# A recurrent attention and mixture-of-experts kernel: three more evictions move from ScalarE to VectorE in the start-up

## The chip, the cores and the metric

The kernel runs on one core of one Trainium2 chip. The metric is the time of one execution on the device in microseconds (us), as the median of the runs that were timed. Lower is better.

## The reference, cut to what matters

```python
def _attn_ref(r, k, v, w, a, b):          # (4, 8, 768, 40): 32 heads, 768 steps, 40 wide
    for t in range(S):
        y[:, :, t] = np.einsum('bhd,bhde->bhe', rt, state)
        Sa = np.einsum('bhde,bhe->bhd', state, at)
        state_decay = state * wt[:, :, None, :] - np.einsum('bhd,bhe->bhde', Sa, bt)
        state = state_decay + np.einsum('bhd,bhe->bhde', vt, kt)
...
def _moe_ref(x, w_gate, w_output_gate, w1, w2):   # 3072 tokens, 8 experts
    e_idx = np.argmax(x @ w_gate, axis=1)
    for e in range(E):
        mask = e_idx == e
        h = np.maximum(x[mask] @ w1[e], 0.0)
        out[mask] = gate_w[mask, None] * eom[mask, e, None] * (h @ w2[e])
```

The first part is a recurrence over 768 steps for 32 heads, the second part routes each of the 3072 resulting tokens to one of eight experts.

## The kernel before

The 768 steps are cut into 12 chunks of 64 steps. Within a chunk the recurrence is written as a triangular system, so a chunk c goes through three stages.

**Prep(c).** `scan` (line 103) forms running products P and I of the decays with two scans on VectorE (line 116) and squares the decays on ScalarE (line 119, only for a range test). `prep` (line 137) scales the inputs: Av on VectorE or GpSimd (lines 184, 185), KBt on VectorE (line 212), Am from Av (line 201 on ScalarE, line 203 on GpSimd, or by DMA on line 192). Then line 225 multiplies KBt by Am on TensorE into PSUM tiles named pl, of which there are two buffers. For each of two sides (16 head pairs each) there are three groups, g0 = 0, 2 and 4, and so six pl tiles to a chunk. Each pl tile is evicted to SBUF in three pieces: the upper half of N (32 partitions, full rows of 64), the lower half of N (32 partitions, half rows) and LA (line 238). The upper half is on VectorE on line 234 for chunk 0, and on ScalarE on line 236 for all other chunks; the lower half is always on ScalarE, line 236. GpSimd then masks LA (line 240). KBt is also transposed on TensorE (line 163) and copied to KB by ScalarE (line 165); the next chunk's KBt may be written only after that.

**Tinv(c)** (line 251) inverts the triangular blocks of N on VectorE, in a long row of small multiplications and sums. Chunks 0 and 1 are done singly: the stage begins with a transposition of N on line 266 and ends with another on line 330, whose result ScalarE copies to Tc (line 333). From chunk 2 on, two chunks are done at once, from line 271 to line 336.

**Crit(c, q) and tail(c, q)** use Tc for the state update and the output, for two halves q of the heads. Their products on TensorE (lines 379 and 392) alternate with moves from PSUM on ScalarE (line 383) and, for chunks 0 and 1, with two additions on VectorE after each product with Nm (line 405).

The program is written in one stream, in which prep and tinv run ahead of crit. The framework's scheduler then sets the order on each engine from estimates of its own, before anything runs. Each engine takes its queue strictly in that order, so an instruction that waits holds up all behind it. After the attention the experts run, where TensorE is the busiest engine.

Of the kernel before, what the change touches and what calls it, by code (L numbers as in the profile page):

```python
# [49 lines left out]
def pat(x, off, dims):  # L50

    return bass.AP(x.tensor, x.offset + off, [x.ap[0]] + [list(d) for d in dims])


class Att:
# [47 lines left out]
    def scan(s, c):  # L103

        nc, V = s.nc, s.nc.vector
        n = 12 * 2 * 33
        w = s.p1.tile([120, n + 1], F32, name="w")
        V.memset(w[:, n:], 0.0)
        nc.sync.dma_start(out=w[:, 0:n], in_=s.win[c])
        s.D = s.p1.tile([120, 12, 3, C], F32, name="D")  # L110
        s.mark[c] = nc.sync.dma_start(out=s.D, in_=s.din[c]).ins
        P, I = (s.p1.tile([120, 12, 2, 33], F32, name=x) for x in "PI")
        Pf, If = (x.rearrange("p r h t -> p (r h t)") for x in (P, I))
        with s.tc.issue_after(s.mark['t', 0]) if c == 2 else ExitStack():
            for o, d in ((Pf, w[:, 0:n]), (If[:, ::-1], w[:, n:0:-1])):
                V.tensor_tensor_scan(out=o, data0=d, data1=s.rst, initial=0.0, op0=ALU.mult, op1=ALU.add)
        wq = pat(w, 1, [(33, 24), (1, 32)])
        with s.tc.issue_after(s.mark['n', 0]) if c == 1 else ExitStack():
            nc.scalar.activation(out=wq, in_=wq, func=AF.Square, bias=s.wb, accum_out=s.wsq[:, c:c + 1])
        rq = s.p1.tile([120, 24], F32, name="rq", bufs=2)  # L120
        V.reciprocal(out=rq, in_=P[:, :, :, 32])
        I3 = I.rearrange("p r h t -> p (r h) t")
        V.tensor_tensor(out=I3, in0=I3, in1=rq.unsqueeze(2).broadcast_to([120, 24, 33]), op=ALU.mult)
        s.Q = P, I, rq
# [12 lines left out]
    def prep(s, c):  # L137
# [45 lines left out]
        with s.tc.issue_after(s.mark['r', 0]) if c == 1 else ExitStack():  # L183
            (g if c > 1 else V).tensor_tensor(out=Av[:, :, 0:33], in0=a[:, :, 0:33], in1=I[:, :, 1, ::-1], op=ALU.mult)
            (g if c > 1 else V).tensor_tensor(out=Av[:, :, 33:64], in0=a[:, :, 33:64], in1=P[:, :, 0, 1:32], op=ALU.mult)
        with s.tc.issue_after(s.mark['n', 0]) if c == 1 else ExitStack():
            nc.scalar.copy(out=Av[:, :, 64:66], in_=P[:, :, :, 32])
        Ag = Av.rearrange("p (a g) t -> p a g t", a=2)
        if c and c != 2:
            for j in range(3):  # L190
                r, n = slice(40 * j, 40 * j + 40), 6 if j < 2 else 4
# [26 lines left out]
        for side in range(2):  # L218
            Am = s.Am[:, side]
            yield  # L220
            for g0 in range(0, 6, 2):
                pl = s.ps.tile([128, 2, 3, C], F32, name="pl", tag="pl" if c or g0 == 0 else "tl", bufs=2 if c or g0 == 0 else 3)
                nj = 3 if g0 < 4 else 2
                for i in range(2):
                    nc.tensor.matmul(pl[:, i, 0:nj], KBt[:, 6 * side + g0 + i].rearrange("p n t -> p (n t)"), Am[:, g0 + i:g0 + i + 6 * nj - 5:6, 0:64],  # L225
                                     start=True, stop=True)
                pv = pl.rearrange("p g j t -> p j g t")
                for h in range(2):
                    r = slice(64 * side + 32 * h, 64 * side + 32 * h + 32)
                    n = C - 32 * h  # L230
                    nn = pat(N[r], C * g0, [(6 * C, nj), (C, 2), (1, n)])
                    pn = pv[64 + 32 * h:96 + 32 * h, 0:nj, :, C - n:]
                    if c == 0 and not h:
                        V.tensor_scalar(out=nn, in0=pn, scalar1=-1.0, scalar2=None, op0=ALU.mult)
                    else:
                        s.mark['n', c] = nc.scalar.activation(out=nn, in_=pn, func=AF.Copy, scale=-1.0).ins  # L236
                la = pat(LA[64:128, side], 66 * g0, [(396, nj), (66, 2), (1, 64)])
                nc.scalar.activation(out=la, in_=pv[0:64, 0:nj], func=AF.Copy, scale=-1.0)  # L238
                for i in range(2):
                    g.affine_select(out=la[:, :, i], in_=la[:, :, i], pattern=[[0, nj], [1, C]], base=0, channel_multiplier=-1,  # L240
                                    compare_op=ALU.is_gt, fill=0.0)
                yield
# [344 lines left out]
class Moe:  # L587
# [346 lines left out]
    def experts(s, ctx, verdict):  # L934
# [21 lines left out]
        def unit(e, t0, nt, prep):  # L956

            for _ in s.expert(nt, W[e], T[e, t0], lambda: s.hp, ps1, ps2) if (e, t0) != (0, 0) else s.E0:
                next(prep, None)
            for _ in prep:  # L960
                pass
# [199 lines left out]
```

## Time and profile before

| | |
|---|---|
| median of 3 runs | 682.52 us (681.66 to 682.61) |
| the profiled execution's own time | 678.98 us |
| span of its trace, first to last instruction | 677.2 us |
| TensorE, matmul busy | 630.9 us (93%) |
| VectorE busy | 464.9 us (69%) |
| ScalarE busy | 340.2 us (50%) |
| GpSimd busy | 233.8 us (35%) |

The page cuts the span into 40 slices of 17 us. In the first 20 or so VectorE is mostly at 6 to 9 tenths and in the later ones at 4 to 6; the attention fills the first 427 us and the experts the rest. The granted TensorE clock is full but for slices 2 to 5, and one each in the middle and at the end. Shares over the whole span mix these stages, so the change has to be read from the first 135 us, where it lies.

In the views, PE is TensorE (PEld its weight load), DVE is VectorE, ACT is ScalarE, POOL is GpSimd and SP the queue that issues most DMAs.

### The profile page before, as it was taken

Reading aid. Unit: us, or ns where it says so; the run is one execution under the profiler, and the core shown is the slowest. Engines: PE = TensorE matmul, PEld = TensorE weight load, DVE = VectorE, ACT = ScalarE, POOL = GpSimd, SP = SyncE. Lnnn points to the kernel's source line nnn. Section 1 sums busy time; section 2 is a strip of 40 time slices with the busy share of each in tenths; the row PEclk is TensorE's granted clock in tenths of the full one; section 3 lists DMA queues with packets and bytes.
Section 4 is the critical chain, followed back from the end, with each engine's and each line's share of the span. In section 5 each row is a group of like instructions: output and inputs, shape, how many; then the busy total and the mean of one; then the engine's idle time right before and its main releaser. Section 6 shows DMA issues by size and latency. Waiting matters only on the chain. (4 is left out here: it accounts for less than half of the span.)

```text
span 677.2 us, 21154 instructions
## 1 busy us (share of the span) xinstructions
PE 630.9 (93%) x8871; PEld 564.3 (83%) x8871; DVE 464.9 (69%) x911; ACT 340.2 (50%) x783; POOL 233.8 (35%) x337
## 2 busy tenths in 40 slices
PE   7787988898999999989999889899999999999996
PEld 6475877787988888878889779799999999999985
DVE  8868689969986997699399654374774545654231
ACT  2577762784378357637743354253573435343120
POOL 9655321341144258314204111335342333211112
PEclk9667999999999999999999979999999999999999
DMA  5995763276346726643224752263774344431001
GB/s 141 179 184 132 175 156 82 78 165 168 98 128 166 157 80 168 173 97 99 83 80 126 194 165 76 58 195 85 213 203 152 115 135 134 150 103 34 19 11 32
DMA packets 56305, 84.45 MB, mean 125 GB/s; under 512 B 26848, under 2 KB 43515, under 8 KB 54763
## 3 DMA queue, kind: packets, MB, share of 16 engines
q1 hardware_dynamic: 52331, 74.05, 42.3%
q0 software_dynamic: 3872, 8.97, 4.7%
q8 instruction: 72, 1.18, 0.7%
q14 instruction: 30, 0.25, 0.1%
HBM read 67.59 MB, written 8.96 MB: 113 GB/s over the span
## 5 line engine op out<-in xcount | busy, mean ns | idle before, releaser
L863 DVE SCALAR_TENSOR_TENSOR hl<-ph,hh 128x480 fp32r<-128x480 f32 (+1 forms) x74 | 41.3, 567 | 65.4 <-ACT hh L862 65.3
L862 ACT ACTIVATE hh<-ph 128x480 fp32r<-128x480 f32 (+1 forms) x74 | 36.7, 501 | 93.5 <-PE ph L858 93.1
L878 POOL DMA_INDIRECT out_dram<-y,ti x32 | 34.3, 1073 | 141.5 <-DVE y L877 80.8
L873 PE MATMUL po<-w2h,hh 128*120 128x320 f32 x256 | 78.3, 311 | 0.2 <-ACT hh L862 0.2
L874 PE MATMUL po<-w2l,hh 128*120 128x320 f32 x256 | 77.6, 309 | 0.0
L858 PE MATMUL ph<-xh,w1h 128*128 128x480 f32 (+1 forms) x222 | 76.1, 347 | 0.3 <-DVE mem L704 0.3
L858 PE MATMUL ph<-xl,w1h 128*128 128x480 f32 (+1 forms) x222 | 75.7, 344 | 0.0
L875 PE MATMUL po<-w2h,hl 128*120 128x320 f32 x256 | 74.9, 308 | 0.0
L225 PE MATMUL pl<-Am,KBt 120*128 120x192 f32 (+1 forms) x288 | 62.9, 352 | 7.7 <-ACT LA L238 6.2
L240 POOL TENSOR_SCALAR_AFFINE_SELECT LA<-LA 64x192 f32<-64x192 f32 x144 | 55.2, 418 | 40.2 <-ACT LA L238 38.8
L383 ACT ACTIVATE As<-pa,hq 128x320 f32<-128x320 f32 x80 | 42.1, 528 | 47.2 <-PE pa L392 36.0
L236 ACT ACTIVATE N<-pl 32x192 f32<-32x192 f32 (+1 forms) x138 | 51.6, 374 | 26.3 <-PE pa L392 12.2
L225 PEld LDWEIGHTS pl<-Am,KBt 120*128 120x128 f32 x288 | 47.1, 205 | 13.4 <-ACT LA L238 8.7
L480 PE MATMUL pY<-KB,M 128*64 128x64 f32 (+1 forms) x768 | 53.3, 225 | 3.0 <-DVE M L468 3.0
L479 PE MATMUL pY<-Sd,R 128*64 128x64 f32 (+1 forms) x704 | 53.9, 227 | 0.0
L392 PE MATMUL pa<-As,Tc 64*32 64x40 f32 x1792 | 51.1, 204 | 2.9 <-ACT As L383 2.1
L730 POOL DMA_INDIRECT tab<-rec,si x24 | 29.9, 1245 | 67.6 <-DMA tab<-rec,si 45.5
L464 PE MATMUL pM<-R,VU 128*128 128x128 f32 x384 | 52.3, 287 | 0.9 <-ACT VU L456 0.8
L480 PEld LDWEIGHTS pY<-KB,M 128*64 128x64 f32 x768 | 46.9, 138 | 6.6 <-DVE M L468 3.4
L838 POOL DMA_INDIRECT xg<-xd,ti x32 | 35.8, 1118 | 44.6 <-PE px L821 32.7
L392 PEld LDWEIGHTS pa<-As,Tc 64*32 64x32 f32 x1792 | 40.3, 112 | 12.8 <-issue 3.8
L858 PE MATMUL ph<-xh,w1l 128*128 128x480 f32 (+1 forms) x148 | 50.7, 344 | 0.0
(198 smaller groups left out, 1571.2 us busy)
## 6 DMA issues: line engine op xcount, KB each, us to landing
D<-in_din_dram SPq DMA_DIRECT2D x12, 1080.0 KB
st<-in_w_dram SPq DMA_DIRECT2D x16, 512.0 KB
st<-in_w_dram SPq DMA_DIRECT2D x16, 480.0 KB
XS<-in_vt_dram SPq DMA_DIRECT2D x24, 256.0 KB
XU<-in_vt_dram SPq DMA_DIRECT2D x24, 256.0 KB
VU<-in_vl_dram SPq DMA_DIRECT2D x24, 208.0 KB
w<-in_win_dram SPq DMA_DIRECT2D x12, 371.2 KB
st<-in_w_dram SPq DMA_DIRECT2D x16, 256.0 KB
```

Source lines behind the costliest of these rows:

```text
L225: nc.tensor.matmul(pl[:, i, 0:nj], KBt[:, 6 * side + g0 + i].rearrange("p n t -> p (n t)"), Am[:, g0 + i:g0 + i + 6 * nj - 5:6, 0:64], sta ...
L236: s.mark['n', c] = nc.scalar.activation(out=nn, in_=pn, func=AF.Copy, scale=-1.0).ins
L240: g.affine_select(out=la[:, :, i], in_=la[:, :, i], pattern=[[0, nj], [1, C]], base=0, channel_multiplier=-1, compare_op=ALU.is_gt, fill=0.0)
L383: s.mark['as'] = nc.scalar.activation(out=x, in_=pa, func=AF.Copy, scale=s.hq[:, h:h + 1]).ins
L392: nc.tensor.matmul(pa[o + w:o + w + 32, i], m(p)[o:o + 64], x[o:o + 64, i, :], start=start, stop=True, tile_position=(o, o + w), skip_grou ...
L464: nc.tensor.matmul(pM[:, i], VU[:, h0 + i].rearrange("p n t -> p (n t)"), R[:, :, h0 + i], start=True, stop=True)
L479: nc.tensor.matmul(o, R[:, side, i, :], Sf[:, 40 * i:40 * i + w], start=True, stop=False)
L480: s.mark['y'] = nc.tensor.matmul(o, Ms[i // 4][:, i % 4, side, :], Kf[:, k:k + w], start=not c, stop=True).ins
L858: nc.tensor.matmul(ph, l, r, start=(i == 0), stop=(i == 7))
L873: nc.tensor.matmul(po, hh[f][:, ts_], w2h[:, f], start=(f == 0), stop=False)
L874: nc.tensor.matmul(po, hh[f][:, ts_], w2l[:, f], start=False, stop=False)
L875: nc.tensor.matmul(po, hl[f][:, ts_], w2h[:, f], start=False, stop=(f == 7))
```

## The change

The condition on line 233 is widened: the upper halves of N are evicted by VectorE for all six tiles of chunk 0 as before, and now also for the three tiles of chunk 1's second side (side 1). The two other edited lines write the same condition in another form and give the same marks.

```diff
-                    if c == 0 and not h:
+                    if not h and (c == 0 or c == 1 and side >= 1):
                         V.tensor_scalar(out=nn, in0=pn, scalar1=-1.0, scalar2=None, op0=ALU.mult)
                     else:
                         s.mark['n', c] = nc.scalar.activation(out=nn, in_=pn, func=AF.Copy, scale=-1.0).ins
```

Three instructions change engine, but the scheduler lays out everything after them anew. The order on all engines differs from chunk 1's second side to about chunk 5, and is the same again afterwards. Three places matter for what follows.

The first is VectorE's queue around chunk 1's second side. The rows with N from pl in 128 columns (32x3x128, 32x2x128) are upper halves; line 266 starts chunk 1's tinv; lines 121 and 123 belong to chunk 2's scan. Before:

```order
L121 RECIPROCAL rq<-P 120x24
L123 TENSOR_TENSOR I<-I,rq 120x792
L108 MEMSET w 120x1
L405 TENSOR_TENSOR As<-As,pa 32x320 x2
L266 STREAM_TRANSPOSE tmpf<-N 128x16x32
L267 TENSOR_SCALAR tmpf<-tmpf,hm 128x256
L268 SCALAR_TENSOR_TENSOR Ns<-tmpf,hm 128x16x16
L276 TENSOR_TENSOR tmpf<-Tt,Ns 128x2
```

And now:

```order
L121 RECIPROCAL rq<-P 120x24
L234 TENSOR_SCALAR N<-pl 32x3x128
L123 TENSOR_TENSOR I<-I,rq 120x792
L234 TENSOR_SCALAR N<-pl 32x3x128
L108 MEMSET w 120x1
L405 TENSOR_TENSOR As<-As,pa 32x320 x2
L234 TENSOR_SCALAR N<-pl 32x2x128
L266 STREAM_TRANSPOSE tmpf<-N 128x16x32
L267 TENSOR_SCALAR tmpf<-tmpf,hm 128x256
L268 SCALAR_TENSOR_TENSOR Ns<-tmpf,hm 128x16x16
L212 TENSOR_TENSOR KBt<-D,P 120x24x32
L212 TENSOR_TENSOR KBt<-D,I 120x24x32
```

The three evictions stand among chunk 2's scan work, each waiting for its product, and chunk 2's KBt has moved ahead of the tinv's first steps.

The second is ScalarE's queue in the same place. The rows 32x3x2x32 and 32x2x2x32 are lower halves, the last group's being 32x2x2x32; line 201 writes a part of Am for chunk 2. Before:

```order
L119 ACTIVATE w,wsq<-w,wb 120x24x32
L383 ACTIVATE As<-pa,hq 128x320
L181 ACTIVATE rs,rqm<-rq 120x24
L236 ACTIVATE N<-pl 32x3x128
L236 ACTIVATE N<-pl 32x3x2x32
L238 ACTIVATE LA<-pl 64x3x2x64
L236 ACTIVATE N<-pl 32x2x128
L236 ACTIVATE N<-pl 32x2x2x32
L238 ACTIVATE LA<-pl 64x2x2x64
L201 ACTIVATE Am<-Av,hj 120x2x6x64
```

And now:

```order
L119 ACTIVATE w,wsq<-w,wb 120x24x32
L383 ACTIVATE As<-pa,hq 128x320
L181 ACTIVATE rs,rqm<-rq 120x24
L236 ACTIVATE N<-pl 32x3x2x32
L238 ACTIVATE LA<-pl 64x3x2x64
L236 ACTIVATE N<-pl 32x3x2x32
L238 ACTIVATE LA<-pl 64x3x2x64
L201 ACTIVATE Am<-Av,hj 120x2x6x64
L165 COPY KB<-pt 128x3x160
L236 ACTIVATE N<-pl 32x2x2x32
L238 ACTIVATE LA<-pl 64x2x2x64
L383 ACTIVATE As<-pa,hq 128x320
```

The upper halves are gone, and line 201 with one copy of KB has moved ahead of the last group's lower half.

The third is VectorE's queue ahead of line 271, where the tinv of chunks 2 and 3 begins. Before:

```order
L123 TENSOR_TENSOR I<-I,rq 120x792
L108 MEMSET w 120x1
L482 TENSOR_TENSOR x<-pY,WT 128x320
L271 STREAM_TRANSPOSE Ns<-N 128x32x32
L276 TENSOR_TENSOR tmpf<-Tt,Ns 128x4
L405 TENSOR_TENSOR As<-As,pa 32x320 x2
```

And now:

```order
L482 TENSOR_TENSOR x<-pY,WT 128x320
L121 RECIPROCAL rq<-P 120x24
L123 TENSOR_TENSOR I<-I,rq 120x792
L108 MEMSET w 120x1
L405 TENSOR_TENSOR As<-As,pa 32x320 x2
L271 STREAM_TRANSPOSE Ns<-N 128x32x32
L276 TENSOR_TENSOR tmpf<-Tt,Ns 128x4
```

One pair of additions of line 405 has moved from behind line 271 to ahead of it. Between the later pairs of lines 271 and 336 VectorE's queue holds the same instructions as before.

## Rows read from the trace of the kernel before

**Rows 1.** Windows: stretch, busy us (count) by engine, PEclk, DMA share, GB/s.
```profile
47.00:66.00 19.00, 12.55 (x215) 10.21 (x217) 17.92 (x37) 14.88 (x39) 12.89 (x19) 0.84 0.66 150
66.00:87.00 21.00, 20.70 (x329) 17.27 (x325) 10.81 (x16) 16.38 (x43) 7.41 (x16) 0.98 0.62 159
87.00:134.00 47.00, 39.32 (x883) 33.86 (x882) 45.60 (x89) 24.92 (x63) 11.30 (x23) 1.00 0.42 107
```

**Rows 2.** Timeline of VectorE, first tinv of a pair: start, us, instruction, [idle before].
```profile
87.17 1.98 DVE L271 STREAM_TRANSPOSE Ns<-N 128x1024 f32<-128x1024 f32 x1 [5.45 <-ACT N L236]
...
89.38 0.99 DVE L405 TENSOR_TENSOR As<-As,pa 32x320 f32<-32x320 f32 x2
...
131.92 2.09 DVE L336 STREAM_TRANSPOSE Tc<-Tt 128x1024 f32<-128x1024 f32 x1
133.89 0.94 DVE L212 TENSOR_TENSOR KBt<-D,P 120x768 f32<-120x768 f32 x1
```

**Rows 3.** Groups by line and form, VectorE, 17 to 60 us: busy us, mean ns.
```profile
L234 DVE TENSOR_SCALAR N<-pl 32x384 f32<-32x384 f32 x4 | 2.1, 549 | 0.1
...
L234 DVE TENSOR_SCALAR N<-pl 32x256 f32<-32x256 f32 x2 | 0.8, 415 | 0.4 <-PE pl L225 0.4
```

**Rows 4.** The same of ScalarE, 17 to 100 us, with idle time before.
```profile
L238 ACT ACTIVATE LA<-pl 64x384 f32<-64x384 f32 x16 | 7.8, 484 | 0.2
...
L236 ACT ACTIVATE N<-pl 32x384 f32<-32x384 f32 x12 | 5.8, 483 | 4.7 <-PE pl L225 4.4
L236 ACT ACTIVATE N<-pl 32x192 f32<-32x192 f32 x16 | 5.2, 324 | 1.0 <-DVE N L234 0.8
...
L165 ACT COPY KB<-pt 128x480 f32<-128x480 f32 x8 | 4.5, 556 | 0.6 <-PE pt L163 0.5
...
L236 ACT ACTIVATE N<-pl 32x128 f32<-32x128 f32 x8 | 2.2, 271 | 0.1
```

**Rows 5.** Timeline, all engines, where chunk 1's tinv begins.
```profile
45.13 0.92 POOL L185 TENSOR_TENSOR Av<-D,P 120x372 f32<-120x372 f32 x1 [1.27 <-DMA R<-in_rl_dram]
...
46.12 1.16 POOL L240 TENSOR_SCALAR_AFFINE_SELECT LA<-LA 64x128 f32<-64x128 f32 x4
...
46.92 0.97 DVE L405 TENSOR_TENSOR As<-As,pa 32x320 f32<-32x320 f32 x2 [1.56 <-PE pa L392]
...
47.37 0.97 POOL L184 TENSOR_TENSOR Av<-D,I 120x396 f32<-120x396 f32 x1
...
47.92 1.11 DVE L266 STREAM_TRANSPOSE tmpf<-N 128x512 f32<-128x512 f32 x1
...
48.37 0.94 ACT L201 ACTIVATE Am<-Av,hj 120x768 f32<-120x768 f32 x1
```

**Rows 6.** Timeline, all engines, chunk 1's tinv to its end.
```profile
48.44 3.77 POOL L203 TENSOR_SCALAR Am<-Av,hj 120x768 f32<-120x768 f32 x2
...
50.83 0.54 DVE L276 TENSOR_TENSOR tmpf<-Tt,Ns 128x18 f32<-128x18 f32 x1
...
56.58 1.79 DVE L116 TENSOR_TENSOR_SCAN P<-w,rst 120x792 f32<-120x792 f32 x1
...
58.41 0.94 ACT L119 ACTIVATE w<-w,wb 120x768 f32<-120x768 f32 x1 [2.41 <-DVE P L116]
...
61.16 1.65 PE L225 MATMUL pl<-Am,KBt 120*128 120x192 f32 x4 [4.40 <-ACT LA L238]
...
64.44 1.08 DVE L330 STREAM_TRANSPOSE tmpf<-Tt 128x512 f32<-128x512 f32 x1
```

**Rows 7.** Timeline, VectorE and ScalarE, chunk 3's prep.
```profile
72.37 0.96 DVE L212 TENSOR_TENSOR KBt<-D,P 120x768 f32<-120x768 f32 x1 [0.17 <-PE pt L163]
...
79.99 0.94 ACT L119 ACTIVATE w<-w,wb 120x768 f32<-120x768 f32 x1 [0.30 <-DVE P L116]
```

**Rows 8.** Windows of 2 us, TensorE alone: busy us (count), granted clock, DMA share.
```profile
58.00:60.00 2.00, 0.00 (x0) 0.98 0.83 184
60.00:62.00 2.00, 0.84 (x3) 0.50 0.69 204
```

More of the change, by code (lines that the diff above doesn't have):

```diff
@@ L117, in scan @@
         wq = pat(w, 1, [(33, 24), (1, 32)])
-        with s.tc.issue_after(s.mark['n', 0]) if c == 1 else ExitStack():
+        with s.tc.issue_after(s.mark['n', c - 1]) if c in (1,) else ExitStack():
             nc.scalar.activation(out=wq, in_=wq, func=AF.Square, bias=s.wb, accum_out=s.wsq[:, c:c + 1])
@@ L185, in prep @@
             (g if c > 1 else V).tensor_tensor(out=Av[:, :, 33:64], in0=a[:, :, 33:64], in1=P[:, :, 0, 1:32], op=ALU.mult)
-        with s.tc.issue_after(s.mark['n', 0]) if c == 1 else ExitStack():
+        with s.tc.issue_after(s.mark['n', c - 1]) if c in (1,) else ExitStack():
             nc.scalar.copy(out=Av[:, :, 64:66], in_=P[:, :, :, 32])
```

## The prediction

> **What bounds the kernel now.** I read the windows first, by stage, since the page's busy shares mix the attention with the experts. From 87 to 134 us VectorE is busy 45.60 of 47 us, while TensorE, ScalarE and GpSimd have 8 us or more to spare [rows 1]. VectorE's timeline then shows why: this is the tinv of chunks 2 and 3, from line 271 at 87.17 to the end of line 336 at 134.01, and the next KBt stands directly behind it [rows 2]. Ahead of line 271 VectorE was idle for 5.45 us until ScalarE's last eviction of N. So the attention goes in turns: a prep that ends with ScalarE's evictions, a tinv that VectorE's queue sets, the next prep. The experts follow the attention. What the change is worth is therefore how much earlier or later line 336 of chunks 2 and 3 ends; all behind it has VectorE's queue with the same instructions, and moves by about as much. ScalarE's and VectorE's idle time away from these two places costs nothing.
>
> **The change part by part.** The moved work itself is small. VectorE takes on 2 x 0.549 + 0.415 = 1.51 us [rows 3]. ScalarE loses 2 x 0.483 us for the two wide tiles and, in proportion to the columns, some 0.35 for the narrow one, 1.3 us together [rows 4]. A lower half still follows its upper half: in chunk 0 ScalarE's lower halves waited 0.8 us for VectorE's upper ones [rows 4], since both write the same tile. VectorE had the room: before the additions at 46.92 it was waiting for TensorE for 1.56 us [rows 5]. Each of the three now waits on VectorE for its product; queued behind the first is chunk 2's line 123, whose taker is GpSimd's line 184, not due before 46.7 (below). Taken alone I cost the move at nothing; without that room it would cost its 1.5 us.
>
> *Start of chunk 1's tinv.* Line 266 needs all of N, so also the last lower half. In ScalarE's new queue that half stands behind line 201 and one copy of KB. Line 201 needs GpSimd's line 184. GpSimd's line 185 began at 45.13 after a wait for a load [rows 5], which the change does not touch; it ends at 46.05, two selections of 0.29 each (four took 1.16) bring GpSimd to 46.7, and line 184 takes 0.97, so to 47.7. Line 201 takes 0.94, to 48.7, the copy 0.56, to 49.2, the lower half 0.27 [rows 4], to 49.5. Line 266 began at 47.92, so it comes 1.6 us late. Behind it are ScalarE's moves for crit(0,0), which gain nothing from the shorter evictions for the same reason.
>
> *End of chunk 1's tinv.* From 47 to 66 us VectorE was busy 17.92 of 19 us [rows 1], and between line 266 and the end of line 330 at 65.52 [rows 6] the new queue holds the same instructions in another order. So line 330 ends at 65.52 + 1.6 = 67.1.
>
> *The wait for chunk 3's scan.* Before, ScalarE waited 2.41 us until 58.41 for the scan P, with chunk 2's evictions queued behind, and TensorE waited 4.40 us for those until 61.16 [rows 6]. In the new queue the scan stands sooner behind line 266, but two additions of line 405 (0.97, [rows 5]) go ahead of it. From 49.5: line 266 with 1.11 [rows 5] and two steps of about half that, KBt 2 x 0.96 [rows 7], three small ones of some 0.2, the scan I 1.8, the additions and one sum 1.2, the scan P 1.8 (1.79, [rows 6]): 59.3. I take this stall as 0.9 us worse; its bounds are 0 and 1.6.
>
> *Chunk 3's prep.* Before, KBt began at 72.37 [rows 7], 6.85 us after line 330, when the last transposition was out of the way. In ScalarE's new queue one wide eviction group (0.483 + 0.324 + 0.484 = 1.3, [rows 4]) and one move of about 0.5 stand ahead of the copy of Tc and no longer behind it: 6.85 - 1.8 = 5.0, so KBt may start at 67.1 + 5.0 = 72.1. VectorE has two mask multiplications ahead of it and starts it at about 73.1, 0.7 late. But then the scans of chunk 4 follow at once: 73.1 + 1.9 + 3.6 = 78.6, where ScalarE's line 119 began at 79.99 [rows 7] after that scan. ScalarE needed 87.17 - 79.99 = 7.18 us from there to the last N; now one wide group (1.3) and a small copy (0.2) more stand in that stretch: 78.6 + 8.7 = 87.3. Line 271 comes at 87.3, 0.1 to 0.2 late. Bounds: if VectorE catches up the 1.6 us, the scans end at 77.0 and line 271 comes at 85.7, 1.4 early; if all the lateness passes, 1.6 late. I take +0.2, nearest to the worked chain.
>
> *The pair of additions.* One pair of line 405, 0.99 us, leaves the tinv of chunks 2 and 3 [rows 2] and goes into the idle 5.45 us ahead of line 271. That takes 0.99 us off a stretch where VectorE is the bound. It holds as long as the pair's product is there by 86.3; otherwise it delays line 271 and the gain is 0.
>
> Sum: +0.2 - 1.0 = -0.8 us, with bounds -2.4 and +1.6. The profiled execution took 678.98 us, 3.5 below the median of the runs; on it the sum gives 678.2, on the median **681.7**.
>
> *GpSimd beside VectorE.* Line 276 at 50.83 took 0.54 us for 18 elements to a partition, as long as an eviction of 384 [rows 3], and it ran beside GpSimd's line 203, 3.77 us for two [rows 6]. In the new order KBt comes up at about 51.7, when the second multiplication of line 203 has some 1.1 us to go (48.4 plus a first one of 1.6, two selections and one of 2.2). I take no hold for it, as the row shows one of less than 0.54. [...]
>
> **The rivals.** [...]
>
> [...]
>
> *C, nothing is passed on (682.5).* The change does not shorten ScalarE's part where it counts, as each lower half waits for its upper half anyway, and VectorE's stretches absorb the rest.
>
> [...]
>
> **How the numbers follow.** Forecast 0.35, A 0.25, B 0.20, C 0.12, D 0.08. A measurement of this kernel can tell 0.2%, 1.37 us, from no change. Faster by more: A, and the early tenth of the forecast's spread, 0.35 in all. Slower by more: B and a little of D, 0.22. Within: 0.43. The likeliest case alone spans 680.6 to 683.0. The range takes in A's and B's centres and most of their spread: 679.3 to 685.0, with 0.08 to 0.1 left out at either end.
>
> **What would show it.** In the changed kernel's trace: three rows of line 234 between 42 and 48 us; line 266 at about 49.5, after an idle stretch that a ScalarE eviction ends, and line 201 starting when line 184 ends; line 330 ending near 67; line 271 near 87.3 with a pair of line 405 just before; from there 45.8 instead of 46.8 us to the end of line 336. [...] I am wrong altogether if line 336 of the later pairs does not move with the first.

## The result: slower by 0.6%

The changed kernel takes **686.07 us** (median of 6 runs, 685.36 to 688.16); the kernel before took 682.56 us beside it (6 runs, 681.13 to 683.16). The ratio is 1.0060, 95% interval 1.0045 to 1.0076 (here and below a ratio leaves out the runs over 1.5% above the fastest of their kernel, while a median takes in all, so the two can differ a little). The prediction was 681.7 with a range to 685.0, so the time lies 1.1 us above the range, and on the other side of no change than the forecast. The profiled execution took 685.39 us (span 683.6) against 678.98 (span 677.2). The two profiles are thus 6.4 us apart in span where the medians are 3.5 apart: the profile of before was a quick one of its kernel, that of after 0.7 us under its median.

The three evictions stand where the change puts them. VectorE's timeline of the changed kernel, with start, us, instruction and [idle before] (answers [rows 3, 5]):

```profile
42.01 0.56 DVE L234 TENSOR_SCALAR N<-pl 32x384 f32<-32x384 f32 x1 [1.30 <-PE pl L225]
...
44.01 0.56 DVE L234 TENSOR_SCALAR N<-pl 32x384 f32<-32x384 f32 x1 [0.27 <-PE pl L225]
...
46.44 0.42 DVE L234 TENSOR_SCALAR N<-pl 32x256 f32<-32x256 f32 x1
49.72 1.09 DVE L266 STREAM_TRANSPOSE tmpf<-N 128x512 f32<-128x512 f32 x1 [2.85 <-ACT N L236]
```

They are done at 46.86, and VectorE then waits 2.85 us for ScalarE. The timeline of GpSimd and ScalarE says for what:

```profile
47.01 0.97 POOL L184 TENSOR_TENSOR Av<-D,I 120x396 f32<-120x396 f32 x1
...
48.01 0.94 ACT L201 ACTIVATE Am<-Av,hj 120x768 f32<-120x768 f32 x1 [1.53 <-POOL Av L184]
48.85 0.54 ACT L165 COPY KB<-pt 128x480 f32<-128x480 f32 x1
49.41 0.27 ACT L236 ACTIVATE N<-pl 32x128 f32<-32x128 f32 x1
```

Line 201 waits for GpSimd, and the last lower half stands behind it and a copy. Line 266 starts 1.80 us later than at 47.92. From there to the end of chunk 1's tinv VectorE's timeline reads (answers [rows 6]):

```profile
51.31 1.09 DVE L268 SCALAR_TENSOR_TENSOR Ns<-tmpf,hm 128x256 f32<-128x256 f32 x1
52.61 0.96 DVE L212 TENSOR_TENSOR KBt<-D,P 120x768 f32<-120x768 f32 x1 [0.21 <-DMA w<-in_win_dram]
...
55.82 1.87 DVE L116 TENSOR_TENSOR_SCAN I<-w,rst 120x792 f32<-120x792 f32 x1 [0.82 <-ACT Wp L216]
58.96 1.81 DVE L116 TENSOR_TENSOR_SCAN P<-w,rst 120x792 f32<-120x792 f32 x1
62.50 0.87 DVE L276 TENSOR_TENSOR tmpf<-Tt,Ns 128x50 f32<-128x50 f32 x1
...
63.64 0.70 DVE L276 TENSOR_TENSOR tmpf<-Tt,Ns 128x72 f32<-128x72 f32 x1
...
68.25 1.11 DVE L330 STREAM_TRANSPOSE tmpf<-Tt 128x512 f32<-128x512 f32 x1
```

Line 330 ends at 69.36, 3.84 us later than before. In the windows between line 266 and that end, VectorE was busy 18.01 of 19.64 us, against 17.04 of 17.60 before: 1.07 us more of waiting and 0.97 more of work. The same engine around the first tinv of a pair (answers [rows 2, 7]):

```profile
75.47 0.95 DVE L212 TENSOR_TENSOR KBt<-D,P 120x768 f32<-120x768 f32 x1
...
89.04 0.99 DVE L405 TENSOR_TENSOR As<-As,pa 32x320 f32<-32x320 f32 x2 [6.02 <-PE pa L392]
90.14 1.99 DVE L271 STREAM_TRANSPOSE Ns<-N 128x1024 f32<-128x1024 f32 x1
...
134.17 2.10 DVE L336 STREAM_TRANSPOSE Tc<-Tt 128x1024 f32<-128x1024 f32 x1
136.44 0.96 DVE L212 TENSOR_TENSOR KBt<-D,P 120x768 f32<-120x768 f32 x1 [0.17 <-PE pt L163]
```

Chunk by chunk the distance to before is +1.80 at line 266, +3.84 at the end of line 330, +2.97 at line 271, +2.26 at the end of line 336, +4.5 at the end of the last line 336 and +6.4 at the end of the span. TensorE's clock fell in other places. Windows of TensorE: busy us (count), granted clock, DMA share, GB/s (answers [rows 8]):

```profile
48.00:50.00 2.00, 0.36 (x2) 1.00 0.86 154
50.00:52.00 2.00, 1.85 (x36) 0.71 0.78 172
52.00:54.00 2.00, 2.00 (x32) 0.50 0.64 170
...
62.00:64.00 2.00, 0.66 (x2) 0.50 0.52 176
64.00:66.00 2.00, 2.00 (x11) 0.50 0.07 14
66.00:68.00 2.00, 2.00 (x20) 0.52 0.00 0
...
112.00:116.00 4.00, 3.64 (x59) 0.53 0.02 4
```

TensorE did next to nothing from 48 to 50 us (0.36 busy), until ScalarE had done the late line 201 and the copy of KB behind it, and its granted clock went to 0.71 and then 0.50 in the windows behind that. The window of before at the same place:

```profile
48.00:50.00 2.00, 1.05 (x34) 1.00 0.99 179
```

There it stayed at 1.00 until the gap at 58 to 60 [rows 8]. (The slices of before with the clock below full are given above as 2 to 5; by the page they are 2 to 4, 17 to 68 us.)

### The profile page after: what moved, and what is told of

The parts are those of the page before. It is cut to its first block, busy times and chain, and to the rows that moved or that the text cites. A ratio compares the mean times of both kernels' runs of the same rounds, so it can differ in the third digit from the quotient of the medians.

```text
span 683.6 us, 21158 instructions
## 1 busy us (share of the span) xinstructions
PE 633.9 (93%) x8871; PEld 566.4 (83%) x8871; DVE 467.6 (68%) x914; ACT 337.7 (49%) x780; POOL 234.2 (34%) x337
## 5 line engine op out<-in xcount | busy, mean ns | idle before, releaser
L225 PE MATMUL pl<-Am,KBt 120*128 120x192 f32 (+1 forms) x288 | 60.5, 342 | 6.1 <-ACT LA L238 5.4
L236 ACT ACTIVATE N<-pl 32x192 f32<-32x192 f32 (+1 forms) x135 | 50.1, 371 | 24.3 <-PE pa L392 10.9
L225 PEld LDWEIGHTS pl<-Am,KBt 120*128 120x128 f32 x288 | 45.2, 199 | 11.4 <-ACT LA L238 7.6
```

## Experiments

Two theories stood at the start. *The work*: the three evictions cost VectorE something. *The order*: what costs is the new layout of the queues, and within it either the stall behind line 201 or the rest. To tell them apart, kernels with a chosen order were built: a table lists the traced instructions of each engine from chunk 1's second side to about chunk 5, and each is queued behind the one named before it. Such an edge sets the issue order alone.

```diff
+def pin(tc):
+    ins = {i.name: i for i in tc.nc.cur_bb.bb.instructions}
+    ...
+        for a, b in zip(q, q[1:]):
+            tc.add_manual_dep(ins[b], a, mybir.DependencyInfo(mybir.DependencyClass.NoSync, mybir.DependencyReason.DATA),
+                              reason="order")
-        flag = nc.values_load(fi, min_val=0, max_val=1 << 20,
+        pin(tc); flag = nc.values_load(fi, min_val=0, max_val=1 << 20,
```

Each batch ran on one chip with its own runs of the kernel before (medians 683.36, 680.53, 681.16 and 679.51 us); ratios are to those. In the fragments of the table below, 443, 451 and 459 are the upper halves, 444, 452 and 460 the lower ones, 461 the last LA, 574 line 201, 472 the first copy of KB and 694 a move of line 383.

**The work in the old order (x1).** ScalarE's row of the table loses the upper halves, VectorE's gains them; nothing else differs from before.

```diff
-573 443-445 506 604 570 451-453 459-461 574 466 472 476 694
+573 444-445 506 604 570 452-453 460-461 574 466 472 476 694
-382 504-505 508-509 743 645-646 513
+382 504-505 508 443 509 451 743 645-646 459 513
```

> The three evictions are on VectorE as in the changed kernel, but every other instruction of every engine stands in the order of the kernel before. If the order is what costs (either the stall behind line 201 or the rest of the order): line 266 at 47.0 to 48.0, line 330 ends at about 65.5, the time is that of the kernel before within 1.4 us, 681.2 to 683.9. If the moved work itself costs: 685 to 687, as changed.

Measured 682.62 us, ratio 0.9985 (0.9962 to 1.0008). So the moved work and a table of the old order together cost nothing that these runs can tell.

**The new order with the old work (x2).** The reverse: the changed kernel's order with the upper halves back on ScalarE.

```diff
-444-445 452-453 574 472 460-461 694
+443-445 451-453 574 472 459-461 694
```

> The three evictions are back on ScalarE, each right ahead of its lower half, and every other instruction of every engine stands in the order of the changed kernel. If the order costs: 685 to 687, line 266 at 49.5 or later and line 330 ending near 69. If the moved work costs: 681.2 to 683.9.

Measured 690.61 us, ratio 1.0116 (1.0089 to 1.0143). The order costs, with the moved work taken out of it. The ratio is above those of the changed kernel (1.0060, and 1.0071 in y4), but these were taken on other chips, and its interval meets that of y4; in its trace line 266 came at 50.85.

**Line 201 put back (x3).**

```diff
-444-445 452-453 574 472 460-461 694
+444-445 452-453 460-461 574 472 694
```

> The changed kernel, with only line 201 and the first copy of KB put back behind the last lower half of N and its LA on ScalarE; all else in the changed kernel's order. If the stall behind line 201 is the cause: line 266 at 47.5 to 48, no fall of the clock at 50 us, line 330 ends at 65.5 to 66.5 and the time is 681 to 683.5. If the rest of the order is the cause: line 266 comes earlier, but line 330 or line 271 as late as changed, and the time is 684.5 to 687.

Measured 690.89 us, ratio 1.0095 (1.0066 to 1.0124): no better, and above both ranges that were expected. The stall is gone and the stage is not shorter. VectorE's timeline of x3:

```profile
47.52 1.09 DVE L266 STREAM_TRANSPOSE tmpf<-N 128x512 f32<-128x512 f32 x1 [0.34 <-ACT N L236]
...
51.88 0.96 DVE L212 TENSOR_TENSOR KBt<-D,P 120x768 f32<-120x768 f32 x1 [2.24 <-PE pt L163]
52.75 0.95 DVE L212 TENSOR_TENSOR KBt<-D,I 120x768 f32<-120x768 f32 x1
55.17 1.81 DVE L116 TENSOR_TENSOR_SCAN I<-w,rst 120x792 f32<-120x792 f32 x1 [0.91 <-DMA w<-in_win_dram]
...
67.58 1.09 DVE L330 STREAM_TRANSPOSE tmpf<-Tt 128x512 f32<-128x512 f32 x1
```

Line 266 comes at 47.52, and VectorE waits the gain off in front of KBt, which must not be written before TensorE's transpositions of chunk 1's KBt are done, and in front of the scan. In the new order KBt and the scans stand ahead of most of the tinv's small steps, so this wait holds up the tinv; from line 266 to the end of line 330 it takes 21.15 us.

**Line 201 ahead in the old order (x4).**

```diff
-443-445 506 604 570 451-453 459-461 574 466 472 476 694
+443-445 506 604 570 451-453 574 472 459-461 466 476 694
```

> The kernel before, with only line 201 and the first copy of KB put ahead of the last eviction of N on ScalarE. If the stall behind line 201 is the cause: line 266 comes at about 50 and the time is 685 to 687. If the rest of the order is the cause: line 266 comes as late, but the time stays within 1.4 us of the kernel before, 681.2 to 683.9.

Measured 685.09 us, ratio 1.0025 (1.0002 to 1.0048): 1.7 us by the medians. In its trace line 330 ends at 68.24, 2.7 late, behind this start of line 266:

```profile
50.89 1.10 DVE L266 STREAM_TRANSPOSE tmpf<-N 128x512 f32<-128x512 f32 x1 [2.37 <-ACT N L236]
```

So the stall by itself costs between 0.1 and 3.3 us. By the number 685.09 is in the range that stood for the stall; but the ranges were made for a before of 682.5, and against its own runs of before (683.36) it lies between the two: more than nothing, and less than the whole loss.

**Fills (y1, y2, y3).** Products of zeros that nothing reads, on TensorE where it waits: 18 in the old order ahead of line 225 at 61 us (y1; y3 with the moved evictions), 22 in the new order's four waits between 47 and 63 us (y2).

```diff
-        with s.tc.issue_after(s.mark['pt']):
+        with s.tc.issue_after(s.mark['pt']) if n == 5 else ExitStack():
-        solve(As3, 1)
+        c or q or s.keep(18); solve(As3, 1)
```

> The kernel before, its order held, with 18 products of zeros (512 columns, bf16) put into TensorE's wait of 4.40 us ahead of line 225 at 61.16 us; nothing reads them. If the granted clock between 60 and 90 us is what scatters the runs and what sets the two orders apart: the clock stays at 1.00 from 47 to 90 us, line 271 comes at 85 to 87 in every run, the time is 678 to 682 and the runs scatter less than those of before. If the order of the queues alone decides: the time is that of before within 1.4 us and the scatter stays.

> The changed kernel, its order held, with 22 such products in TensorE's four waits between 47 and 63 us (6 ahead of line 163 at 49.44, 1 ahead of the next, 4 ahead of line 392 at 58.98, 11 ahead of line 225 at 63.34). If the clock sets the two orders apart: no fall between 48 and 90 us and the time within 1.4 us of the filled old order. If the order of the queues decides: line 266 at 49.7 and line 330 at 67 or later all the same, and 3 us or more above the filled old order.

> The three evictions on VectorE, all else in the order of the kernel before, with the same 18 products ahead of line 225 at 61 us. Either theory: as the filled old order within 1.4 us, since the moved work costs nothing; if the work had a price that the clock's scatter hid, it is above it by 1.5 us or more.

Measured: y1 683.44 us (1.0029, 0.9998 to 1.0060), y2 683.58 (1.0040, 1.0013 to 1.0066), y3 681.92 (1.0031, 1.0000 to 1.0061). In y1 the fall was not taken away but moved. Its TensorE timeline:

```profile
57.10 4.06 PE L135 MATMUL fk<-rst,zh 120*32 120x512 bf16 x18
61.70 0.92 PE L225 MATMUL pl<-Am,KBt 120*128 120x192 f32 x4 [0.54 <-ACT LA L238]
...
65.30 0.81 PE L430 MATMUL pS<-XU,KB 128*40 128x40 f32 x16
68.11 0.63 PE L163 MATMUL pt<-ident,KBt 120*128 120x120 f32 x4 [2.00 <-ACT LA L238]
```

The products at 61 now took 0.92 us at a clock of 1.00, and no longer 1.65 at 0.50, TensorE came to the next wait sooner, and the clock was at 0.50 from 70 to 82 us, where TensorE has no idle time (2.00 us busy in every window of 2). From the end of line 330 to line 271 y1 took 27.01 us, where before took 21.65; TensorE's window of y1 for it:

```profile
65.80:92.81 27.01, 24.84 (x306) 0.75 0.50 126
```

So y1 could not settle the question it was meant for. In y2 the clock was 0.96 from 45.00 to 68.49 us and 1.00 from there to 134.96, and the kernel was 3.6 us under the changed one on the same chip (y4, below), yet not down at before. With y1, the filled old order that it was to be set beside, y2 is level (0.14 us), as the clock theory asked; since y1's clock fell, that speaks for neither theory. The median granted clock of y2's runs was 0.975, above the 0.971 of the runs of before on that chip, so a lower mean clock is not what y2 lost by.

**The changed kernel again (y4).** No edit.

> The changed kernel once more, beside the others on the same chip: 685 to 690, 3 to 6 us above before. In a profile of a run at 690 the clock theory has TensorE at 0.50 for 10 us more between 60 and 90 us than in the run at 685.4; if the order alone decides, the windows of the clock are the same in both.

Measured 687.17 us, ratio 1.0071 (1.0037 to 1.0105). The profiled run has the lower clock for 12.3 us between line 330 and line 271, and that stretch is 25.68 us long, where the first profile of the same kernel has none and 20.78. TensorE's window for it:

```profile
69.53:95.21 25.68, 23.87 (x318) 0.76 0.47 123
```

Yet both executions have a span of 683.6 us: line 271 came 5.1 us later in the second, and behind the last line 336 it had these back (295.74 us against 300.94). The profiled run took 685.35 us, so what a run at 690 looks like was not seen.

**The order cut in two (z1, z2, z6).** All with the moved evictions: the new order up to the end of chunk 1's line 330 and the old behind it (z1), the reverse (z2), and the new order from line 271 only (z6). In ScalarE's row z1, and in VectorE's rows z2 and z6 (982 and 983 are line 271 and the first step behind it, 1178 and 1179 a pair of line 405), against x1:

```diff
-573 444-445 506 604 570 452-453 460-461 574 466 472 476 694
+573 506 604 570 444-445 452-453 574 472 460-461 694 466 476
-1496 1088 982-983 1178-1179 984
+1088 976-977 1496 1178-1179 982-986
-1496 1088 982-983 1178-1179 984
+1496 1088 982 1178-1179 983-986
```

> The moved evictions, with the changed kernel's order on every engine up to the end of chunk 1's tinv (line 330, about 68 us) and the order of the kernel before from there. If the new order up to line 330 (line 201's stall, TensorE idle at 48 us) makes the clock stay low: 685 to 688, mean clock 0.955 to 0.962. If the order of chunk 3's prep or of the tinv behind it does it: 681 to 684, mean clock 0.968 to 0.973.

> The moved evictions, with the order of the kernel before up to the end of line 330 of chunk 1 and the changed kernel's order behind it. If the order up to line 330 is the cause: as before within 1.4 us, clock 0.968 to 0.973. If the order behind it is: 685 to 688, clock 0.955 to 0.962.

> The moved evictions, with the order of the kernel before up to the start of the first tinv of a pair (line 271, about 87 us) and the changed kernel's order behind it. If what lies behind line 271 costs (a second fall of the clock at 112 to 120 us stood only in the changed kernel): 684 to 687. If it is all ahead of line 271: as before within 1.4 us, or 0.7 under it, as the stretch from line 271 to the end of line 336 was 0.7 us shorter in the changed kernel.

Measured: z1 684.55 us (1.0066, 1.0042 to 1.0090), z2 683.14 (1.0035, 1.0013 to 1.0058), z6 684.87 (1.0076, 1.0045 to 1.0107). The times of z1 and z2 lie between the two ranges that were expected of each: neither half of the order is shown to be the whole cause. By the medians the part up to line 330 costs 3.4 us, the part behind it 2.0. The median granted clocks of their runs, 0.963 and 0.964, also lie between what the two theories asked, and below the 0.970 of before; by the slope that the runs of before show (last section) 0.006 less clock goes with some 3.3 us, an estimate, so z2's loss may be the clock's and not the queues'. z6 decides nothing: its mixture makes a wait that neither kernel has (KBt at 94.74 behind 2.36 us for line 163), and its first tinv of a pair takes 50.88 us.

**More fills, in both orders (y5, y7, y8).** y5 is y1 with 8 more products ahead of line 163 at 68 us (into a PSUM buffer of another tag), y7 the same with the moved evictions, y8 is y2 once more.

```diff
-        c or q or s.keep(18); solve(As3, 1)
+        c or q or s.keep(26); solve(As3, 1)
-        fl = s.ps.tile([32, 512], F32, name="fk", tag="pS")
+        fl = s.ps.tile([32, 512], F32, name="fk", **(dict(tag="pS") if n == 5 else dict(tag="tl", bufs=3)))
```

> The kernel before, its order held, with 18 products of zeros ahead of line 225 at 61 us and 8 more ahead of line 163 at 68 us, where the first fill left TensorE idle for 2.00 us and the clock fell. If the clock in the stretch from line 330 to line 271 is what cost 3 to 7 us there: 1.00 from 48 to 90 us, the stretch 20.5 to 22 us, and the time 677 to 680, under before by 1 to 3 us. If the clock only goes along with something else: the stretch stays at 25 or more and the time at 682 to 685.

> The same fills, with the three evictions on VectorE. Within 1 us of y5 by either theory.

> The changed order with its 22 fills once more, beside y5. If clock and order share the cost: 3 to 5 us above y5, of which 1 to 3 stand in the trace ahead of line 330 and the rest behind line 336. If the clock was all: within 1.4 us of y5.

Measured: y5 680.14 us (1.0023, 0.9997 to 1.0049), y7 680.87 (1.0012, 0.9983 to 1.0041), y8 684.20 (1.0066, 1.0034 to 1.0097). The windows of y5's TensorE show the clock held where it was wanted:

```profile
48.00:65.00 17.00, 14.75 (x244) 1.00 0.66 146
65.00:87.00 22.00, 21.38 (x321) 1.00 0.60 153
```

and those of y8 nearly so:

```profile
48.00:68.00 20.00, 18.29 (x290) 1.00 0.60 139
68.00:90.00 22.00, 19.49 (x301) 0.92 0.56 144
```

Up to line 330 both run at full clock, and there y8 is 2.85 us behind y5 (68.33 against 65.48; y2, filled like y8, 68.49, and y7, filled like y5, 65.60). That is the order, with the fills that go with each. As a whole y8 is 4.1 us above y5 by the medians, 2.9 by the ratios. How much of this is the clock still is open: the median granted clock of y8's runs was 0.9715, of y5's 0.976, and by the same slope that goes with some 2.5 us, an estimate. No version beat the kernel before: y5 holds the clock and is level with it, and the gain of 1 to 3 us that was expected of it did not come.

The stages of the profiled executions, from VectorE's timelines (us; "low" is the time at a granted clock of 0.50 between the end of line 330 and line 271, worked out as (1 - granted clock) / 0.5 times the stretch, an estimate that takes the clock to be at 1.00 or 0.50; no window of 2 us reads lower):

| kernel | L266 at | to L330's end | to L271 | low | to L336's end | to last L336's end |
|---|---|---|---|---|---|---|
| before | 47.92 | 17.60 | 21.65 | 1.3 | 46.84 | 244.10 |
| after | 49.72 | 19.64 | 20.78 | 0.0 | 46.13 | 246.39 |
| y4, after again | 49.21 | 20.32 | 25.68 | 12.3 | 46.54 | 246.11 |
| x1, work, old order | 48.17 | 17.84 | 28.63 | 18.9 | 46.09 | 246.98 |
| x2, new order, old work | 50.85 | 19.11 | 22.42 | 3.6 | 45.71 | 247.36 |
| x3, 201 behind | 47.52 | 21.15 | 26.08 | 13.0 | 46.67 | 248.40 |
| x4, 201 ahead | 50.89 | 17.35 | 21.73 | 1.3 | 46.46 | 243.93 |
| y1, old, one fill | 48.77 | 17.03 | 27.01 | 13.5 | 46.73 | 245.37 |
| y2, new, filled | 50.34 | 18.15 | 20.77 | 0.0 | 45.70 | 245.52 |
| y3, work, old, one fill | 48.22 | 17.77 | 25.55 | 10.2 | 46.17 | 244.00 |
| z1, new, then old | 49.23 | 19.80 | 23.80 | 9.0 | 46.15 | 245.48 |
| z2, old, then new | 48.49 | 17.72 | 23.25 | 0.0 | 46.57 | 246.39 |
| z6, new from L271 | 48.78 | 17.50 | 22.06 | 2.2 | 50.88 | 246.55 |
| y5, old, held | 48.19 | 17.29 | 21.59 | 0.0 | 46.69 | 245.46 |
| y7, work, old, held | 48.10 | 17.50 | 21.66 | 0.0 | 46.81 | 247.06 |
| y8, new, filled | 50.12 | 18.21 | 21.61 | 3.5 | 45.68 | 246.97 |

From line 266 to the end of line 330 the seven profiles with the new order there take 18.15 to 21.15 us, the nine with the old one 17.03 to 17.84: no overlap. In the two later stages the orders overlap.

## Why the prediction was wrong, step by step

**What bounds the kernel: right in kind.** The attention goes in turns, and the loss can be read off at the ends of the turns.

**The moved work at nothing: right.** x1 shows it, and y7 beside y5 (680.87 against 680.14 us).

**Line 266 at 49.5: right (49.72), and for the reason given.** Line 201 started when line 184 ended, and the copy and the half followed. x4 makes the same delay in the old order.

**"The same instructions in another order, so line 330 ends 1.6 late": the step that failed.** I took the length of 17.6 us over because VectorE was nearly always busy there. It became 19.64. Four rows, set beside these of before, make 2.4 us of it:

```profile
49.52 0.48 DVE L268 SCALAR_TENSOR_TENSOR Ns<-tmpf,hm 128x256 f32<-128x256 f32 x1
...
53.99 0.28 DVE L276 TENSOR_TENSOR tmpf<-Tt,Ns 128x50 f32<-128x50 f32 x1
...
54.54 0.28 DVE L276 TENSOR_TENSOR tmpf<-Tt,Ns 128x72 f32<-128x72 f32 x1
54.74 1.80 DVE L116 TENSOR_TENSOR_SCAN I<-w,rst 120x792 f32<-120x792 f32 x1
```

The scan I waited 0.82 us for ScalarE's copies of Wp, for which TensorE's transpositions came late, behind its idle time at 48 us and at a clock of 0.71 and 0.50 from 50 to 54; in y8, at 1.00, the scan waits for nothing, and the stretch is 18.21. Line 268 took 1.09 us where 0.48 had done. And two steps of line 276 moved into the time of GpSimd's two-input multiplications (lines 185 and 184): 50 elements in 0.87 (0.28 before) and 72 in 0.70 (0.28 before). The rest went both ways: the step of 18 elements, 0.54 before, took 0.15, the second pair of line 314 0.82 where it had taken 1.37, and several small steps 0.1 to 0.2 more. x3 shows that the step was wrong in principle too: a queue that puts KBt and the scans first hangs on their suppliers and no longer on line 266. The same instructions have the same length only if the same ones wait.

**Scan P for line 119 at 59.3: off by that step.** The scan ended at 60.77 and line 119 began at 60.80, with TensorE's product behind it at 63.34 (before 61.16): the stall was 2.2 us worse, where I had 0.9 and a bound of 1.6.

**Chunk 3's prep: right in its length.** From the end of line 330 to line 271 I had 20.2 us, measured 20.78 (before 21.65); KBt came 6.1 us behind line 330, worked out at 6.0. So line 271 at 90.14 in place of 87.3 is the earlier 2.3 us handed on and 0.6 more. That the length came out is in part luck: it went with a clock that stood at 1.00 in this execution, and in y4, the same kernel, the stretch took 25.68.

**The pair of line 405 out of the tinv: right in kind, too large by the other profiles.** 46.13 us after 46.84, and 45.68 in y8 after 46.69 in y5: 0.7 and 1.0 us, for 0.99 predicted. But over all profiles (z6 left out) this stage takes 45.68 to 46.67 us in the new order and 46.09 to 46.84 in the old one, 0.35 us apart in the mean. Its product did come too late for its place (89.04, after 6.02 us of waiting), but ScalarE's last eviction ended at 90.11, so it delayed nothing.

**"All behind it moves by about as much": failed by 2.3 us between the two profiles, and not settled by the others.** From line 336 on VectorE has the same instructions, but the scan of chunk 5 waited 0.97 us for Wp where it had waited 0.33; all eight profiles with the new order there show 0.96 or 0.97, the eight with the old one 0.29 to 0.33. VectorE's timeline of y8:

```profile
139.63 1.81 DVE L116 TENSOR_TENSOR_SCAN I<-w,rst 120x792 f32<-120x792 f32 x1 [0.96 <-ACT Wp L216]
141.94 1.80 DVE L116 TENSOR_TENSOR_SCAN P<-w,rst 120x792 f32<-120x792 f32 x1
```

and of y5:

```profile
136.80 1.81 DVE L116 TENSOR_TENSOR_SCAN I<-w,rst 120x792 f32<-120x792 f32 x1 [0.33 <-ACT Wp L216]
138.52 1.78 DVE L116 TENSOR_TENSOR_SCAN P<-w,rst 120x792 f32<-120x792 f32 x1
```

In y8 a step of line 468 also stands between the two scans, which start 2.31 us apart and not 1.72. What this costs is not shown: to the end of the last line 336 the new order takes 245.52 to 248.40 us, the old 243.93 to 247.06, 1.4 apart in the mean; and of the filled kernels y2 and y8 (245.52, 246.97) are level with y5 and y7 (245.46, 247.06). z2 has this order alone and costs 2.0 us (0.13% to 0.58%), with the lower clock told of above.

Summed as the prediction did, from the profiles: +1.8 (line 266) + 2.0 (to line 330) - 0.9 (to line 271) - 0.7 (the pair) = +2.2 where I had -0.8, and another 2.3 to the last line 336, which I had at 0 and of which the other profiles bear out 1.4 in the mean. The experts' 1.9 us between the two profiles is not the change: the stretch behind the last line 336 lies between 295.7 and 301.6 us over all the profiles, in either order.

**The range and the chances.** The range takes in A and B, and D has a chance of 0.08. A and B are estimates of how long TensorE's granted clock stays below full, D is one of how long GpSimd holds VectorE's KBt; no run shows the lengths that their times were worked out from. What the runs showed in their place: line 271 comes at 87.07 us at the earliest (y5), where the lower bound asked for 85.7. In the first profile of the changed kernel the clock was at 1.00 again from 68 us; in y4 it was 0.76 from 69.53 to 95.21 us, 12.3 us of this at the lower clock, with line 271 at 95.21. So a longer fall, on B's side of the range, happens in some executions of this kernel, and the loss by the queues comes on top.

**No hold on KBt: right.** It ran in 0.96 us beside line 203. The steps that ran longer beside GpSimd were small ones. GpSimd's timeline of the changed kernel beside the rows of VectorE above:

```profile
51.22 2.21 POOL L203 TENSOR_SCALAR Am<-Av,hj 120x768 f32<-120x768 f32 x1
...
62.36 0.91 POOL L185 TENSOR_TENSOR Av<-D,P 120x372 f32<-120x372 f32 x1 [3.48 <-DVE w L108]
63.22 0.98 POOL L184 TENSOR_TENSOR Av<-D,I 120x396 f32<-120x396 f32 x1
```

The step of 50 elements began at 62.50 and ended at 63.37, 0.1 us behind line 185; that of 72 ended at 64.34, 0.14 behind line 184. But line 268 ended 1.0 us before the second multiplication of line 203 did, and KBt beside it lost nothing. Line 268 takes 1.09 us in y2, y8 and z1 too. In the changed kernel it begins 0.09 us behind the start of that multiplication; where it begins 0.86 us (x3) or 1.08 us (before) behind the start of one of line 203, it takes 0.48. What makes these steps longer is not shown.

**What stays open.** That the order costs and the moved work does not is shown by x1 and x2, and that the new order lengthens the stretch to line 330 by 16 profiles. How the rest divides is not. With fills, y8 stays 2.9 to 4.1 us above y5, and a part of this can be the clock. Without fills the changed kernel lost 3.5 us on one chip and on another 6.6 by the medians, 4.8 by the ratio. Whether the rest on the second is the clock was not settled by an experiment; what speaks for it is that the mean granted clock of the changed kernel's runs there was 0.959 against 0.971 in the median. What the fills cost by themselves in either order was not tried, nor which instruction behind line 336 costs how much.

## To carry to other kernels

Where a scheduler lays out the queues anew, the cost of an edit can be that of the new order (here 0.9985 for the work alone in x1, 1.0116 for the order alone in x2): hold the old order by explicit edges and time the edit in it, then the new order without the edit. A stretch in which an engine is busy keeps its length in another order only if what stands first in the queue has its inputs by then (17.60 us before, 19.64 in the changed kernel, 21.15 in x3), so for each instruction that moves ahead look up its supplier's end in the trace, and carry the wait on to everything queued behind it. One profile shows one course of TensorE's clock (two of the changed kernel had 0.0 and 12.3 us at the lower clock between lines 330 and 271, and took 20.78 and 25.68 us there): look at several executions before a stage's length is used to a microsecond.

## What the runs showed of the hardware

**The stretch between line 330 and line 271 goes with its time at the lower clock.** Over the 16 profiled executions of the table its length follows 21.3 us + 0.37 times the time at a granted clock of 0.50 in it (correlation 0.96, where 1 would be a straight line), in both orders. With the clock held in the old order it is 21.59 us (y5) and 21.66 (y7), with one wait less filled 27.01 (y1) and 25.55 (y3). x1 is the plainest case, with VectorE's queue of before but for three evictions. Its TensorE window from line 330 to line 271:

```profile
66.00:94.60 28.60, 28.46 (x337) 0.67 0.46 119
```

and its VectorE timeline:

```profile
64.91 1.10 DVE L330 STREAM_TRANSPOSE tmpf<-Tt 128x512 f32<-128x512 f32 x1
...
94.64 1.97 DVE L271 STREAM_TRANSPOSE Ns<-N 128x1024 f32<-128x1024 f32 x1 [5.61 <-ACT N L236]
```

TensorE was busy throughout at a mean of 0.67, and line 271 came 7.5 us later than in the profile of before.

**The same kernel scatters with it.** Over 117 runs of the kernel before, on four chips, the time and the mean granted clock of a run go together with a correlation of -0.82 (each chip's medians taken off): 0.01 less clock goes with 5.5 us more. Where a fall lands differs from execution to execution of one kernel: in the first profile of the changed kernel the clock was below full from 50 to 56 and from 60 to 68 us, and 1.00 from 69.36 to 90.14; in the second it was 0.70 from 45.00 to 69.53 and 0.76 from 69.53 to 95.21.

**With one wait filled the fall came behind the next.** In y1 and y3 TensorE waited 2.00 and 2.01 us ahead of line 163 at 68; in y1 the clock was 1.00 up to 68 us and 0.50 from 70 to 82. The stretch to line 271 had 13.5 us (y1) and 10.2 us (y3) at the lower clock; with that wait filled too it read 1.00 (y5, y7). In the old order without fills it had 1.3 us (before), 18.9 (x1) and 1.3 (x4), so how long the clock is low in it differs between executions either way.
